# Unit 0's q and k loaded in fp32 by two hardware queues and cast on VectorE, and its first keys copied by themselves

## The chip, the cores and the metric

The kernel runs on one core of one Trainium2 chip. The metric is the time of one execution on the device in microseconds (us). Times are given as the median of several executions; the profile shows one execution.

## What is computed

Two steps follow each other. First attention without a softmax, over 8 batches, 12 heads, 448 positions and 64 numbers a head; then a feed-forward layer over the 3584 rows that come out:

```python
scores = scale * np.matmul(q, k.transpose(0, 1, 3, 2))     # scale = 1/sqrt(64)
attn = np.maximum(scores, 0.0) ** 2 / S                    # S = 448
x = np.matmul(attn, v)                                     # then (B*S, H*D) = (3584, 768)
r = np.maximum(x @ w_in, 0.0)                              # w_in (768, 2048)
out = (r * r) @ w_out                                      # w_out (2048, 768)
```

All inputs and the output are fp32 in HBM. The kernel computes in fp16 with fp32 sums in PSUM.

## The kernel before

**Tiling.** The attention is cut into 24 units, three to a batch; a unit is four heads. Its q, k and v each lie in SBUF as a tile of 128 partitions by 2 by 448 numbers (`heads`, L80): two of the four heads are on the partition axis, the other two (`hh`) beside each other, and each partition holds seven (`J`) positions. A tile of scores is one of the seven groups of keys of a unit, against all 448 queries.

**Loads.** `load16` (L90) loads q and k of a unit on the queue of POOL, which turns fp32 into fp16 on the way; `load_v` (L97) does so for v, `load_w1` and `load_w2` for the weights. POOL's queue holds nearly all loads of the kernel, in program order: first q and k of unit 0 (L153), then the identity matrix that the transposes need (L155, made on POOL too), then units 1 and 2. The queue of SP has the DMA transposes of units 6 and up and the stores of the output; its first instruction comes at 59.8 us.

**The start.** TensorE (PE) runs ten matmuls on zeros (`warm(10)`, L790), then `pe_transpose(0)` (L791): 14 small transposes for q into one PSUM slot, a VectorE (DVE) copy to qT, one more matmul on zeros, the same for k and kT, and one more matmul on zeros. After that the loop of 11 visits (L792) computes the scores of batch 0. `score` (L246) issues the matmuls of a tile, twice each in this stage, and a Relu on ScalarE (ACT, L258) from PSUM to the tile `at`; DVE squares `at` in place (L371), and `av_round` (L262) multiplies it with v.

**PSUM slots.** `slot` (L194) hands out three buffers in turn, every third being `third`; whoever writes a slot waits until the buffer's last user has been read.

**Order.** Nothing reorders the work: the engines run their instructions in the order in which this program issues them. After the first batch a list of steps and events with planned times (L838 and on) fixes that order when the kernel is built. `pe_transpose` is also called for units 1, 2 (two visits of the first loop), 3 (its copies are put off and called as `later`), 4 and 5 (through `mm_tile` buffers).

Of the kernel before, what the change touches and what calls it, by code (L numbers as in the profile page):

```python
# [10 lines left out]
FP16 = mybir.dt.float16  # L11
FP32 = mybir.dt.float32
# [5 lines left out]
def kernel(  # L18
# [9 lines left out]
    nc = tc.nc  # L28

    B, H, S, D = q.shape  # L30
# [11 lines left out]
    P = 128  # L42
    J = 7
# [21 lines left out]
    x_p = ctx.enter_context(tc.tile_pool(name="xp", bufs=3))  # L65
    g_p = ctx.enter_context(tc.tile_pool(name="gp", bufs=1))
    early = ExitStack()
    q16_p = early.enter_context(tc.tile_pool(name="q16p", bufs=3))

    PSUM = bass.MemoryType.PSUM  # L70
# [9 lines left out]
    def heads(t, n):  # L80
        b, u = divmod(n, NU)
        return t[b].rearrange(
            "(hh u hp) (p j) d -> u (hp p) hh (j d)", hh=2, hp=2, j=J)[u]
# [6 lines left out]
    def load16(n):  # L90
        tq = q16_p.tile([P, 2, J * D], FP16, name="q16", tag="q16")
        tk = q16_p.tile([P, 2, J * D], FP16, name="k16", tag="k16")
        nc.gpsimd.dma_start(out=tq, in_=heads(q, n))
        nc.gpsimd.dma_start(out=tk, in_=heads(k, n))
        q16s[n] = (tq, tk)

    def load_v(n):  # L97
        t = v_p.tile([P, 2, J * D], FP16, name="vt", tag="vt")
        nc.gpsimd.dma_start(out=t, in_=heads(v, n))
        vts[n] = t  # L100
# [12 lines left out]
    def new_qkt():  # L113
        return [qkt_p.tile([P, J, P], FP16, name=nm, tag=nm) for nm in ("qT", "kT")]
# [35 lines left out]
        dst, x, y = ((t1, b12, b11), (t3, b22, b12), (t2, b22, t1), (nt4, b21, t2))[op]  # L150
        nc.vector.tensor_sub(dst[:, c], x[:, c], y[:, c])

    load16(0)  # L153
    ident = const_p.tile([P, P], FP16, name="ident", tag="ident")
    make_identity(nc, ident)  # L155
    zeros = const_p.tile([P, S], FP16, name="zeros", tag="zeros")
    nc.vector.memset(zeros, 0.0)
    junk = const_p.tile([P, 1], FP16, name="junk", tag="junk")
    nc.scalar.activation(out=junk, in_=zeros[:, 0:1], func=AF.Relu)
    load16(1)  # L160
    load_v(0)
    load16(2)
# [31 lines left out]
    def slot(dtype):  # L194
        slot_no[0] += 1
        third = not big and slot_no[0] % 3 == 2 and slot_no[0] < 29
        return (third_p if third else s_p).tile(
            [P, 2, 2048 // mybir.dt.size(dtype)], dtype, name="slot", tag="slot")

    def warm(n):  # L200
        ps = slot(FP32)
        for _ in range(n):
            nc.tensor.matmul(ps[:, 0, 0:S], lhsT=zeros[:, 0:P], rhs=zeros,
                             start=True, stop=True)

    def pe_transpose(n):
        srcs = q16s.pop(n)
        ts = new_qkt()
        ps = None if n > 3 else slot(FP16)

        def copy(i, act=False):
            dst, ps = ts[i].rearrange("p j c -> p (j c)"), pss[i][:, i if n < 4 else 0, 0:J * P]
            if act:
                nc.scalar.activation(out=dst, in_=ps, func=AF.Copy)
            else:
                nc.vector.tensor_copy(dst, ps)

        if n > 3:
            pss = [mm_tile(None, FP16).rearrange("p (i c) -> p i c", i=1) for _ in range(2)]
        else:  # L220
            pss = [ps, slot(FP16) if n == 0 else ps]
        for i, src in enumerate(srcs):
            for j in range(J):
                for hh in range(2):
                    nc.tensor.transpose(  # L225
                        pss[i][64 * hh:64 * hh + 64, i if n < 4 else 0, j * P:(j + 1) * P],
                        src[:, hh, j * D:(j + 1) * D], ident)
            if n == 0:
                copy(i)
                warm(1)  # L230
        qkt[n] = ts
        if n == 3:
            return lambda: (copy(0, True), copy(1))
        if n > 0:
            copy(0, n > 3)
            copy(1)


    xts: dict = {}
# [133 lines left out]
    def visit(tiles, turn=None, lag=2, most=3):  # L373
        now[0] += 1
        for t in tiles:
            if t % J == 0 and t >= NPE * J:
                prefetch(t // J + 2)
        if big:
            for t in tiles[:1]:
                score(t)  # L380
            av_unit()
            for t in tiles[1:]:
                score(t)
            at_pe[0] += 0.19 + 0.19 * len(tiles)
            for i, t in enumerate(tiles):
                square(ats[t], 0.6 + 0.85 * i)
            return
        for t in tiles:
            score(t, 2)
        if turn is not None:  # L390
            pe_transpose(turn)
        flush()
        av_some(lag, most)
        for t in tiles:
            square(ats[t])
        flush()
# [5 lines left out]
    def mm_tile(i=None, dtype=FP32):  # L402
        if i is None:
            mm_no[0] += 1
            i = mm_no[0] % len(big)
        return big[i].tile(
            [P, 2048 // mybir.dt.size(dtype)], dtype, name="mm", tag="mm")
# [381 lines left out]
    NB0 = NU * J  # L789
    warm(10)  # L790
    pe_transpose(0)  # L791
    for i in range(11):  # L792
        visit([t for t in (2 * i, 2 * i + 1) if t < NB0], turn={1: 1, 4: 2}.get(i))
# [9 lines left out]
        if i == 5:  # L803
            load16(5)
            load_w1(3)
            load_v(5)
    later = pe_transpose(3)
    load_v(6)
    load_w2(b11, 0, 0)
# [7 lines left out]
        name="mma", bufs=2, space=PSUM, reuse_waits="tile")))  # L817
# [5 lines left out]
    def some(part):  # L823
# [9 lines left out]
        name="mmb", bufs=2, space=PSUM, side="right", reuse_waits="tile")))  # L833
# [36 lines left out]
    for pr in range(1, B // 2):  # L870
# [3 lines left out]
        for i in range(21):  # L874
            ts = [t0 + 2 * i, t0 + 2 * i + 1]
# [86 lines left out]
```

## Time and profile before

| | us |
|---|---|
| median of 3 runs | 373.85 (373.79 to 373.89) |
| the profiled execution | 373.79 |
| its span in the profile | 372.0 |
| PE busy in the span | 361.2 (97%) |
| DVE busy | 278.6 (75%) |
| ACT busy | 247.6 (67%) |
| POOL busy | 107.6 (29%) |

The span runs from the first to the last instruction of the profile; the 1.79 us between it and the execution's time lie around it. PE is busy nearly throughout, but a matmul that waits in the pipeline counts as busy, so the share alone does not say what sets the end. For that there is the chain of waits: it starts at the last instruction and goes back, at each step, to what released it. Lines of the profile give a start, a length and what ran (engine, line of the kernel, operation, tile written <- tiles read, partitions x elements, type, count); the brackets hold the idle time before it and what ended that.

### The profile page before, as it was taken

Reading aid. Unit: us, or ns where it says so; the run is one execution under the profiler, and the core shown is the slowest. Engines: PE = TensorE matmul, PEld = TensorE weight load, DVE = VectorE, ACT = ScalarE, POOL = GpSimd, SP = SyncE. Lnnn points to the kernel's source line nnn. Section 1 sums busy time; section 2 is a strip of 40 time slices with the busy share of each in tenths; the row PEclk is TensorE's granted clock in tenths of the full one; section 3 lists DMA queues with packets and bytes.
Section 4 is the critical chain, followed back from the end, with each engine's and each line's share of the span. In section 5 each row is a group of like instructions: output and inputs, shape, how many; then the busy total and the mean of one; then the engine's idle time right before and its main releaser. Section 6 shows DMA issues by size and latency. Waiting matters only on the chain.

```text
span 372.0 us, 8794 instructions
## 1 busy us (share of the span) xinstructions
PE 361.2 (97%) x3600; PEld 230.4 (62%) x3600; DVE 278.6 (75%) x518; ACT 247.6 (67%) x370; POOL 107.6 (29%) x128
## 2 busy tenths in 40 slices
PE   7999999999999999999999999999999999999994
PEld 3554444445555778875555588786455689975663
DVE  1886677996766787798975668989956688995442
ACT  2997895786676999876556588886665885532220
POOL 8635431955442354432054145140000000000001
PEclk9999999999999999999999999999999999999998
DMA  7999999999999999998798999591233300002333
GB/s 113 203 205 205 205 204 172 134 172 136 171 171 131 174 100 102 115 107 65 137 125 121 186 154 89 82 116 35 55 82 87 86 0 2 2 0 73 95 90 85
DMA packets 121160, 42.65 MB, mean 115 GB/s; under 512 B 100832, under 2 KB 117760, under 8 KB 121120
## 3 DMA queue, kind: packets, MB, share of 16 engines
q0 software_dynamic: 82912, 23.01, 61.7%
q1 hardware_dynamic: 38048, 18.98, 26.8%
q8 instruction: 28, 0.46, 0.5%
q10 hardware_dynamic: 160, 0.10, 0.1%
q14 instruction: 12, 0.10, 0.1%
HBM read 45.61 MB, written 11.01 MB: 152 GB/s over the span
## 4 chain that ended last, share of the span: by engine, by line
PE 84%; DVE 7%; ACT 5%; issue 2%; DMA 1%; POOL 0%; POOLq 0%; DVEq 0%; ACTq 0%
PE mm L739 31%; PE mm L552 25%; PE mm L422 9%; PE slot L254 9%; PE slot L319 7%; ACT at L258 4%; DVE at L371 2%; DMA k<-in_k_dram 1%; DVE s L608 1%; DVE g L500 1%; PE slot L225 1%; DVE g L493 1%; DVE xt L285 1%; DVE osb L646 1%; DVE g L498 1%
## 5 line engine op out<-in xcount | busy, mean ns | idle before, releaser
L258 ACT ACTIVATE at<-slot 128x896 f16<-128x896 f32 x168 | 146.0, 920 | 27.9 <-PE slot L254 27.9
L371 DVE TENSOR_TENSOR at<-at 128x896 f16<-128x896 f16 x168 | 99.0, 617 | 11.2 <-ACT at L258 11.0
L108 POOL DMA_DIRECT2D qs<-in_q_dram x36 | 35.5, 987 | 115.6 <-DMA qT<-qs 107.7
L739 PEld LDWEIGHTS <-s 128*128 128x128 f16 x440 | 41.3, 98 | 34.2 <-DVE s L608 3.8
L254 PE MATMUL slot<-qT,kT 64*64 64x448 f16 x756 | 57.4, 360 | 1.7 <-ACT at L258 0.9
L552 PEld LDWEIGHTS <-w 128*128 128x128 f16 x576 | 54.3, 98 | 5.2 <-issue 4.3
L552 PE MATMUL mm<-xt,w 128*128 128x224 f16 x432 | 49.0, 259 | 0.0
L739 PEld LDWEIGHTS <-g 128*128 128x128 f16 x336 | 31.7, 98 | 24.1 <-issue 4.7
L552 PEld LDWEIGHTS <-ws 128*128 128x128 f16 x432 | 40.3, 98 | 4.7 <-issue 4.7
L739 PE MATMUL mm<-b,g 128*128 128x384 f16 x224 | 40.7, 326 | 0.0
L739 PE MATMUL mm<-b,s 128*128 128x384 f16 x216 | 39.6, 327 | 1.0 <-DVE s L608 0.9
L422 PE MATMUL mm<-xt,w 128*128 128x448 f16 x192 | 39.8, 354 | 0.0
L646 DVE SCALAR_TENSOR_TENSOR osb<-mm,u 128x384 f32<-128x384 f32 (+1 forms) x30 | 16.2, 542 | 31.2 <-ACT u L641 19.3
L739 PE MATMUL mm<-t,s 128*128 128x384 f16 x224 | 39.4, 326 | 0.0
L108 POOL DMA_DIRECT2D ks<-in_k_dram x36 | 35.4, 985 | 9.3 <-DMA b<-in_moe_w_out_dram 5.8
L254 PEld LDWEIGHTS <-kT 64*64 64x64 f16 x756 | 19.6, 104 | 28.9 <-issue 23.6
L575 POOL DMA_DIRECT2D out_dram<-osb x2 | 1.1, 564 | 121.0 <-DVE osb L646 121.0
L641 ACT ACTIVATE u<-mm 128x384 f32<-128x384 f32 x28 | 13.8, 491 | 32.5 <-PE mm L739 31.3
L552 PE MATMUL mm<-x,ws 128*128 128x224 f16 x288 | 34.1, 259 | 0.0
L319 PE MATMUL slot<-at,vt 64*64 64x448 f16 x588 | 31.9, 350 | 0.2 <-DVE at L371 0.2
L500 DVE TENSOR_TENSOR g<-g 128x896 f16<-128x896 f16 x48 | 29.8, 620 | 1.2
L493 DVE TENSOR_TENSOR g<-mm,m 128x448 f16<-128x448 f32 x36 | 22.2, 620 | 10.7 <-PE mm L552 7.4
(69 smaller groups left out, 392.7 us busy)
## 6 DMA issues: line engine op xcount, KB each, us to landing
out_dram<-osb SPq DMA_DIRECT2D x52, 192.0 KB, 3.0
vt<-in_v_dram POOLq DMA_DIRECT2D x24, 224.0 KB, 6.7
qs<-in_q_dram POOLq DMA_DIRECT2D x36, 112.0 KB, 4.3
ks<-in_k_dram POOLq DMA_DIRECT2D x36, 112.0 KB, 5.4
w<-in_moe_w_in_dram POOLq DMA_DIRECT2D x8, 384.0 KB, 11.9
b<-in_moe_w_out_dram POOLq DMA_DIRECT2D x4, 768.0 KB, 17.2
q<-in_q_dram POOLq DMA_DIRECT2D x6, 224.0 KB, 7.1
k<-in_k_dram POOLq DMA_DIRECT2D x6, 224.0 KB, 7.6
```

What stands on the lines that cost most here:

```text
L108: nc.gpsimd.dma_start(out=t[:, :, hh, :], in_=heads(src, n)[:, hh].rearrange("p (j d) -> p j d", d=D))
L254: nc.tensor.matmul(ps[c, hh, 0:S], lhsT=kT[r, j, c], rhs=qT[r, :, c], start=True, stop=True)
L258: nc.scalar.activation(out=at, in_=ps[:, :, 0:S], func=AF.Relu, scale=SK)
L319: nc.tensor.matmul(ps[64 * hh:64 * hh + 64, hp, 0:S], lhsT=vt[r, hh, j * D:(j + 1) * D], rhs=at[r, hh, :], start=(j == 0), stop=(j == J - 1))
L371: lambda: nc.vector.tensor_mul(at, at, at), 0))
L422: nc.tensor.matmul(cell[0][:, 0:S], lhsT=w1[f // 4][:, m, (f % 4) * P:(f % 4 + 1) * P], rhs=xts[b][:, m, :], start=(m == 0), stop=(m == NM ...
L493: nc.vector.tensor_add(gs(s, hi, right), acc(s, y), keep[s, nm])
L500: due_g.append((t, 0.54, lambda: nc.vector.tensor_mul(g, g, g), b))
L552: nc.tensor.matmul(XY[s][y][:, r * Q:(r + 1) * Q], lhsT=left(k, i0 + 2 * s + r, m), rhs=right(k, m), start=(fresh and r == 0 and m == 0), ...
L641: nc.scalar.activation(out=t, in_=X[0][:, 0:HALF], func=AF.Copy, scale=CO)
L646: nc.vector.scalar_tensor_tensor(out=osb[row][:, c], in0=acc[0][:, 0:cc.stop - cc.start], scalar=CO, in1=keep[nm][:, cc], op0=ALU.mult, op ...
L739: nc.tensor.matmul(acc[0][:, 0:HALF], lhsT=left()[:, f], rhs=right[:, f], start=(fresh and f == 0), stop=(f == KH - 1), skip_group_check=n ...
```

## The change

Three things are changed, all ahead of the first score.

1. POOL no longer loads q and k of unit 0. SP loads q and ACT loads k, each as fp32 into a tile of its own (`raw0`, 128 x 896 numbers, a pool of 3.5 KB a tile and partition), and two DVE copies cast them to the fp16 tiles that the transposes read.
2. For unit 0 the keys are transposed in two parts: the first of the seven groups into one slot, the other six into the next slot, with a DVE copy of 128 columns and one of 768 in place of one of 896. One matmul on zeros behind kT's copy is gone; the number of slots taken is the same.
3. `pe_transpose` is written anew around two inner functions, `turn` and `copy`. For the units after 0 it issues the same instructions as before.

```diff
+    raw0_p = early.enter_context(tc.tile_pool(name="raw0p", bufs=1))
     q16_p = early.enter_context(tc.tile_pool(name="q16p", bufs=3))
...
-    load16(0)
+    raw0 = []
+    for src, nm, eng in ((q, "rq", nc.sync), (k, "rk", nc.scalar)):
+        raw0.append(raw0_p.tile([P, 2, J * D], FP32, name=nm, tag=nm))
+        eng.dma_start(out=raw0[-1], in_=heads(src, 0))
     ident = const_p.tile([P, P], FP16, name="ident", tag="ident")
     make_identity(nc, ident)
     zeros = const_p.tile([P, S], FP16, name="zeros", tag="zeros")
     nc.vector.memset(zeros, 0.0)
     junk = const_p.tile([P, 1], FP16, name="junk", tag="junk")
     nc.scalar.activation(out=junk, in_=zeros[:, 0:1], func=AF.Relu)
+    q16s[0] = [q16_p.tile([P, 2, J * D], FP16, name=nm, tag=nm) for nm in ("q16", "k16")]
+    for t, src in zip(q16s[0], raw0):
+        nc.vector.tensor_copy(t, src)
     load16(1)
...
-            if n == 0:
-                copy(i)
-                warm(1)
...
+        if n == 0:
+
+            pq, pk = slot(FP16)[:, 0], slot(FP16)[:, 0]
+            turn(0, pq)
+            copy(0, pq)
+            warm(1)
+            turn(1, pk, slice(0, 1))
+            copy(1, pk, slice(0, 1))
+            pk = slot(FP16)[:, 0]
+            turn(1, pk, slice(1, J))
+            copy(1, pk, slice(1, J))
+            return None
```

`turn(i, ps, js)` issues the two transposes of each group in `js` for q (i = 0) or k (i = 1) into the slot `ps`; `copy(i, ps, js)` copies those columns to qT or kT. Every line of the kernel behind this start moves down by 20 in the profile of the changed kernel (the Relu of the scores is L278 there, the transposes are L230, the copies L225, the casts L167).

## Prediction

> **What bounds the kernel now.** The chain of waits shows two things. First its summary by engine on the page.
>
> ```profile
> PE 84%; DVE 7%; ACT 5%; issue 2%; DMA 1%; POOL 0%; POOLq 0%; DVEq 0%; ACTq 0%
> ```
>
> TensorE carries 84%. DMA has 1%, which is 4.19 us of 372.0, and that is one step, seen in the same chain in order of time for the first 20 us (start, length, what):
>
> ```profile
> 1.28 0.51 POOL q L93
> ...
> 2.12 4.19 DMA k<-in_k_dram
> 6.32 0.04 issue
> 6.36 0.60 PE slot L225 x14
> ...
> 6.99 0.64 DVE kT L216
> ...
> 7.67 0.60 PE slot L254 x8
> ...
> 8.29 6.66 ACT at L258 x8
> ```
>
> So the run begins with load k, transpose k, copy k, first score, first Relu at 8.29; eight Relus then follow without a pause, and later no transfer stands on the chain. The change edits only what lies before 8.29. If the first Relu moves by x, I let the end move by x: behind it the chain goes from ACT to PE and DVE work that the change leaves in the same order, and from 58 us it is matmul after matmul.
>
> Third, the timeline of the start: what the load step is made of.
>
> ```profile
> 0.74 1.28 ACT L159 ACT_TABLE_LOAD   x1 [0.74 <-PEq L946]
> ...
> 1.16 3.86 PE L203 MATMUL slot<-zeros 128*128 128x448 f16 x10 [1.16 <-DVE zeros L157]
> 1.28 0.85 POOL L93 DMA_DIRECT2D q<-in_q_dram  x1 [0.83 <-POOLq L946]
> ...
> 5.27 0.58 PE L225 MATMUL slot<-ident,q 128*64 128x128 f16 x14 [0.25 <-DMA q<-in_q_dram]
> ...
> 5.89 0.62 DVE L216 COPY qT<-slot 128x896 f16<-128x896 f16 x1 [4.79 <-PE slot L225]
> ```
>
> The ten warming matmuls fill PE to 5.02; q has landed by 5.27, k by 6.31. Fourth, the stages in half microseconds (the last two columns are the DMA share and the GB/s written):
>
> ```profile
> 2.50:3.00 0.50, 0.50 (x2) 0.15 (x1) 0.00 (x0) 0.00 (x0) 0.50 (x2) 1.00 0.79 20
> 3.00:3.50 0.50, 0.50 (x3) 0.28 (x2) 0.00 (x0) 0.00 (x0) 0.42 (x3) 1.00 0.26 7
> 3.50:4.00 0.50, 0.50 (x3) 0.18 (x2) 0.00 (x0) 0.00 (x0) 0.50 (x1) 1.00 0.94 147
> 4.00:4.50 0.50, 0.50 (x3) 0.15 (x1) 0.00 (x0) 0.00 (x0) 0.50 (x2) 1.00 1.24 202
> ```
>
> Bytes come from 2.84 on, at a crawl for 0.65 us, then at 200 GB/s of fp16. The queue wrote 23.01 MB where HBM read 45.61, so that is 400 GB/s of fp32 read. Summing the windows, q's 0.229 MB are written by 4.70 and k's by 5.8; each is usable 0.5 to 0.57 us later.
>
> **The change, part by part.** It removes POOL's two loads of unit 0, adds one load each on SP and ACT, adds two DVE casts, splits the copy of kT in two, and drops one of the 12 warming matmuls. In the built order of all five engines nothing else differs; the spread squares that its description names are not in it.
>
> *When q and k land (T).* SP and ACT are free at 0.70 (ACT's table load starts at 0.74). The trace has no load issued there, but a store from SP:
>
> ```profile
> 358.43 9.57 SPq L575 DMA_DIRECT2D out_dram<-osb  x10
> ...
> 359.20:359.45 0.25, 0.25 (x3) 0.17 (x2) 0.24 (x1) 0.00 (x0) 0.00 (x0) 1.00 0.00 0
> 359.45:359.70 0.25, 0.25 (x4) 0.14 (x2) 0.25 (x1) 0.00 (x0) 0.00 (x0) 1.00 0.70 172
> ```
>
> Issue to first bytes is 1.0 to 1.25 us; POOL's load took 1.56 (1.28 to 2.84). I take 1.15. The slow beginning of the reads is bounded by 0 and 0.65; I take 0.65, since it was seen on loads of these very tensors. The data is twice as large on the SBUF side, 2 x 0.459 MB. At the 400 GB/s that the casting loads read it takes 2.3 us; at 250, a good stretch of stores, 3.7. I take 2.3, the row that reads the same rows of HBM. Landing adds 0.55.
>
> Then the neighbour. POOL now makes the identity first (0.60 us in the trace, 2.84 to 3.44), so it issues unit 1's q at about 1.85 instead of 3.40, and this reaches its full rate 2.2 us later, as unit 0's did (1.28 to 3.5), at 4.05. From 2.5 to 4.05 the two new loads have read 0.62 MB; the remaining 0.30 MB share the engines with a third stream: at two thirds of 400 they take 1.1 us instead of 0.75. Bounds: nothing, if the new loads go first; 0.65, if POOL issues at 1.28. I take 0.35.
>
> T = 0.70 + 1.15 + 0.65 + 2.3 + 0.35 + 0.55 = 5.7 for both. In sum k comes 0.6 earlier than now, q 0.45 later.
>
> The Trainium skill (DMA: Bandwidth & Descriptors, Latency and other measured facts) gives about 0.6 us to the first byte for a load issued by SP or ACT, against the 1.15 from the store row. By the page T would be an estimated 5.15 and the sum below a gain of 0.2 us.
>
> *The casts.* No DVE instruction of the trace reads fp32 from SBUF alone. DVE rows with two fp16 inputs give 617 ns for 896 elements and 949 for 1536: 0.519 ns an element and 152 ns fixed. fp32 from PSUM, 448 in 0.62, is 1.04 an element, so 1.09 us for 896 is the upper bound; 0.38, the fp16 tile of L498 from SBUF, is the lower. From PSUM to SBUF the fp16 price per element halves (617 and 383 less 152: 465 to 231). Halving 1.04 gives 0.62 us. I take that.
>
> POOL writes load descriptors all through this time, so I look for a DVE copy from SBUF beside such an issue:
>
> ```profile
> 121.05 2.28 POOL L108 DMA_DIRECT2D ks<-in_k_dram  x2
> ...
> 121.15 0.68 DVE L593 COPY g<-g 128x2048 f16<-128x2048 f16 x1
> ...
> 158.06 0.46 DVE L498 TENSOR_SCALAR g<-g 128x448 f16<-128x448 f16 x1
> ```
>
> L593 kept its 0.68 while POOL's pair took 2.28 where 1.95 is usual; L498 took 0.46 instead of 0.27 beside a load of v. So DVE pays 0 to 0.2 and POOL about 0.3 a copy. POOL's queue runs 1.5 us ahead of before, which covers that; without the cover it would be 0.6 on loads of units 1 and 2 that no one waits for. I take 0.
>
> The Trainium skill (SBUF — State Buffer, Who interferes with whom) speaks against the change: such a copy and POOL's descriptor writing lock each other out for a whole instruction. Were the casts the ones to wait, an estimated 0.7 us each would come on top.
>
> *From T to the first Relu.* Behind the waiting casts are queued on DVE the copies of qT and kT, on PE the transposes and all scores; ACT's first work waits for those. Cast q T+0.05 to T+0.67; cast k, 0.54 later as back-to-back copies start, to T+1.21. PE transposes q from T+0.71; its copy begins 0.62 later (5.27 to 5.89), T+1.34 to T+1.96; the one pair of k and the warming matmul go under it. The other 12 transposes of k need the PSUM buffer that qT's copy frees: from T+2.0, 0.028 us apart, 0.33. The copy of the first keys (128 elements, 0.22) is done meanwhile. Score at T+2.33, Relu 0.62 later (7.67 to 8.29): T+2.95. Before it was k's landing + 1.98 (6.31 to 8.29). So the chain after the landing grows by 0.97 and break-even is T = 5.34. The second copy of kT (0.55) ends at T+3.13, the second score at T+3.79, when the first Relu (0.83) ends at T+3.78: hidden, but with no slack. The dropped warming matmul (0.2 to 0.4) waited beside kT's copy and saves nothing. ACT's issue of about 0.5 delays its table load to 1.25 to 2.5, still 6 us early; SP has no work before 59 us.
>
> Sum: 5.7 + 2.95 - 8.29 = +0.36 us. The profiled run is 373.79 (span 372.0 and 1.79 around it), 0.06 under the median of 373.85: 374.2 us.
>
> **The rivals.**
>
> *Hardware queues win* (0.17): no slow beginning, or q lands first because SP is served before ACT. For it: the store row shows none. T = 0.70 + 1.0 + 2.3 + 0.5 = 4.5 at best: 7.45 against 8.29, -0.84, 373.0; with 0.35 of sharing 373.4. PE's warming to 5.02 then also holds the transposes (T+0.71 = 5.21, just free).
>
> *Data at the stores' rate* (0.15), the main one on the slower side: at 250 GB/s instead of 400 the same 0.92 MB take 3.7, T = 7.1 with sharing, 6.75 without: +1.4 to +1.8, 375.3 to 375.6. It decides from T = 6.1 on, where the loss passes 0.75 us. Against it: stores write HBM, these loads write SBUF.
>
> *Casts at one element a step* (0.10): 1.09 each moves the copy of qT from T+1.34 to T+2.17: +0.83 more, +1.2, 375.05.
>
> *PE cools down* (0.03): silence from 5.02 to T+0.71 = 6.4 is 1.4 us. After the last matmul, at 367.0, the granted clock fell only at 370.05, so it needs T over 7.3; then 375.5 or more.
>
> **How the numbers follow.** The forecast has 0.55, own range 373.5 to 374.6 (sharing and slow beginning at their ends). 0.2%, 0.75 us, is about what a measurement of this kernel can tell from no change. Faster by more needs nearly the whole best case: 0.10 of the first rival's 0.17. Slower by more: 0.15 + 0.10 + 0.03, and 0.04 of the forecast's tail: 0.32. Within: 0.58. The range for 8 in 10 cuts the worst part of the data rival and the tip of the gain: 373.1 to 375.3.
>
> **What would show it.** In the changed profile: DVE's first cast near 5.75 and 0.62 long; the first Relu near 8.65; DMA windows near 400 GB/s by 2.5, shared from 4. Wrong if the cast starts before 5.0 or after 6.1, takes over 0.8, or if the first Relu's shift does not reach the end.

## The result and the profile after

| | before | after |
|---|---|---|
| median, us | 373.82 (373.78 to 373.89, 4 runs) | 375.18 (374.60 to 375.70, 4 runs) |
| ratio | | 1.0036, 95% interval 1.0018 to 1.0053 |
| profiled execution, us (span) | 373.79 (372.0) | 375.41 (373.6) |

The change makes the kernel slower by 1.36 us, and its runs lie 1.1 us apart where those of before lay within 0.11 (in the larger sets taken beside the runs below, those of before lie 0.55 to 0.87 us apart). The chain by engine hardly moves; the loss is all at the start. First that summary, then the chain of the changed kernel in order of time up to 14 us (start, length, what):

```profile
PE 85%; DVE 7%; ACT 4%; issue 2%; DMA 1%; POOL 0%; POOLq 0%; DVEq 0%; ACTq 0%
```

```profile
0.74 4.71 DMA rq<-in_q_dram
...
5.48 0.90 DVE q L167
6.39 0.72 DVE k L167
7.10 0.60 DVE qT L225
...
7.74 0.53 PE slot L230 x12
8.27 3.11 PE slot L274 x32
11.37 1.08 PE slot L230 x28
12.46 0.53 PE slot L274 x8
...
13.01 1.73 ACT at L278 x2
```

q's load is over at 5.46, and k's, which nothing waits for, at 0.75 + 5.0 = 5.75, 0.56 us ahead of k's old landing at 6.31. That sum is from the list of loads (the last number is the time from issue to landing):

```profile
rq<-in_q_dram SPq DMA_DIRECT2D x1, 448.0 KB, 4.7
rk<-in_k_dram ACTq DMA_DIRECT2D x1, 448.0 KB, 5.0
```

But where the kernel before went straight into eight Relus at 8.29, here 32 score matmuls stand on the chain for 3.11 us. Before, 24 of them took 1.33. The timeline of the same stretch:

```profile
0.74 0.45 SPq L158 DMA_DIRECT2D rq<-in_q_dram  x1
0.75 0.48 ACTq L158 DMA_DIRECT2D rk<-in_k_dram  x1
...
5.48 0.90 DVE L167 CAST q<-rq 128x896 f16<-128x896 f32 x1 [4.38 <-DMA rq<-in_q_dram]
...
6.31 0.80 DVE L167 CAST k<-rk 128x896 f16<-128x896 f32 x1
...
6.44 0.58 PE L230 MATMUL slot<-ident,q 128*64 128x128 f16 x14 [1.39 <-DVE q L167]
...
8.20 3.17 PE L274 MATMUL slot<-qT,kT 64*64 64x448 f16 x32
...
9.14 3.35 ACT L278 ACTIVATE at<-slot 128x896 f16<-128x896 f32 x4 [6.38 <-PE slot L274]
```

and its stages (busy time of PE, of PEld, which is TensorE loading weights, of DVE, ACT and POOL, then granted clock, DMA share and GB/s):

```profile
5.00:6.40 1.40, 0.05 (x1) 0.00 (x0) 0.92 (x2) 0.00 (x0) 1.40 (x3) 1.00 1.21 196
6.40:8.30 1.90, 1.61 (x33) 1.12 (x37) 1.42 (x3) 0.00 (x0) 0.97 (x2) 1.00 1.26 201
8.30:11.70 3.40, 3.40 (x40) 1.37 (x41) 1.81 (x3) 2.56 (x4) 2.71 (x4) 0.50 1.27 203
11.70:13.00 1.30, 1.30 (x42) 0.99 (x41) 0.50 (x1) 0.79 (x1) 0.66 (x1) 0.99 1.26 202
```

TensorE is silent from 5.05 to 6.44, and from 8.30 to 11.72 it is granted half its clock. In the kernel before the clock opened at 4.83, that is, went to full, and fell only at 370.05, behind the last matmul.

Put side by side from the two traces, Relu by Relu: the first four are 0.85 us late, the fifth (13.01 for 11.59) 1.42, and from there to the last ACT instruction the shift stays between 1.41 and 1.42, but for one instruction. So the start passes through to the end whole, and nothing later gains or loses. The remaining 0.2 of the 1.6 us between the spans lies behind the issue of the last stores (368.19 for 366.78); no run here says why.

### The profile page after: what moved, and what is told of

Same layout as the page of the kernel before. It is cut to its first block, busy times and chain, and to the rows that moved or that the text cites. A ratio compares the mean times of both kernels' runs of the same rounds, so it can differ in the third digit from the quotient of the medians.

```text
span 373.6 us, 8797 instructions
## 1 busy us (share of the span) xinstructions
PE 362.5 (97%) x3599; PEld 230.4 (62%) x3599; DVE 280.3 (75%) x521; ACT 247.8 (66%) x370; POOL 105.3 (28%) x126
## 4 chain that ended last, share of the span: by engine, by line
PE 85%; DVE 7%; ACT 4%; issue 2%; DMA 1%; POOL 0%; POOLq 0%; DVEq 0%; ACTq 0%
PE mm L759 31%; PE mm L572 25%; PE slot L274 10%; PE mm L442 9%; PE slot L339 7%; ACT at L278 3%; DVE at L391 2%; DMA rq<-in_q_dram 1%; DVE s L628 1%; PE slot L230 1%; DVE g L520 1%; DVE g L513 1%; DVE xt L305 1%; DVE osb L666 1%; DVE g L518 1%
## 5 line engine op out<-in xcount | busy, mean ns | idle before, releaser
L278 ACT ACTIVATE at<-slot 128x896 f16<-128x896 f32 x168 | 146.0, 920 | 28.8 <-PE slot L274 28.7
L274 PE MATMUL slot<-qT,kT 64*64 64x448 f16 x756 | 58.5, 369 | 0.8 <-ACT at L278 0.6
```

The lines of the kernel that those rows point to most:

```text
L274: nc.tensor.matmul(ps[c, hh, 0:S], lhsT=kT[r, j, c], rhs=qT[r, :, c], start=True, stop=True)
L278: nc.scalar.activation(out=at, in_=ps[:, :, 0:S], func=AF.Relu, scale=SK)
```

## The experiments

The question was how the 1.42 us divide: late data, slow casts, the split, or the clock. In every profile the clock's changes lie 3.41 us apart, or multiples of it, but their place against the kernel's start differs from one profile to the next. So each run tells of its own case, and the medians mix them. Ratios are to runs of the kernel before that were taken beside each run; their medians are 373.97 for the runs with 16 warming matmuls, the split alone and the loads alone, 373.78 for the silence by itself and for q on SP with k on POOL, and 373.84 for the others.

**More warming matmuls.**

```diff
-    warm(10)
+    warm(16)
```

> The changed kernel with 16 warming matmuls in place of 10, so that TensorE is busy until about 6.3 us, when q has been cast. Clock theory: TensorE's silence from 5.04 to 6.44 us makes the clock fall to half from 8.30 to 11.72 us, and this costs 0.3 us up to the first Relu and 0.56 us up to the fifth, 0.87 in all. Then the clock stays up, the first Relu comes near 8.8 us, all later Relus are 0.5 to 0.6 us later than in the kernel before, the time is 374.3 to 374.5 us and the runs agree within 0.2 us. Rival, late data and slow casts alone: the time stays at 375.2 us, with the first Relu at 9.1.

Measured: 374.70 us (374.54 to 375.36), ratio 1.0021 (1.0012 to 1.0031). The median falls by about 0.5 us, though not to 374.4, and the intervals of the two ratios overlap, so the medians alone do not show a gain. In its profile the clock never falls again (all Relus are 0.89 to 0.91 us late, with no jump at the fifth), but it opened only at 6.28:

```profile
1.16 5.71 PE L211 MATMUL slot<-zeros 128*128 128x448 f16 x16 [1.16 <-DVE zeros L162]
...
6.80 0.58 PE L230 MATMUL slot<-ident,q 128*64 128x128 f16 x14
```

With the changed kernel's opening at 4.89 about ten of the sixteen would run slow; here all but the last few did, so the warming itself held q's transposes back from 6.44 to 6.80. A fixed number of matmuls overshoots when the clock opens late.

That filling the silence keeps the clock up is seen in every run's mean granted clock. The two profiles with a fall at the start, the changed kernel's and one below, have 0.995; the kernel before has 0.996 or more in all its runs. Two of the changed kernel's four runs have that value, and none of the 20 runs with 16 warming matmuls here and in the next experiment (0.996 to 1.000).

**The same, with POOL's loads held back.** A write of one column of the fp32 k tile, which must wait for k's cast, stands in POOL's queue behind three loads:

```diff
-    for t, src in zip(q16s[0], raw0):
-        nc.vector.tensor_copy(t, src)
     load16(1)
     load_v(0)
+    for t, src in zip(q16s[0], raw0):
+        nc.vector.tensor_copy(t, src)
+    nc.gpsimd.memset(raw0[1][:, 0, 0:1], 0.0)
     load16(2)
```

> As the run with 16 warming matmuls, and besides POOL holds its loads behind the first three (q, k of unit 1, v of unit 0) until both casts are done, by a write of one column of the fp32 k tile. Lock theory: the casts take 0.62 us each when POOL writes no load descriptors, q's transposes start 0.28 us earlier, the first Relu comes near 8.5 us and the time is 374.1 us. Rival, the cast itself costs 0.8 to 0.9 us: no change against the run with 16 warming matmuls, 374.4 us.

Measured: 374.30 us (374.10 to 375.16), ratio 1.0013 (1.0004 to 1.0022); the profiled run is 374.13. Seven of its eleven runs took 374.10 to 374.33, the other four 374.96 to 375.16; what these four lost is open, since none of them was profiled. Its timeline:

```profile
1.16 5.01 PE L212 MATMUL slot<-zeros 128*128 128x448 f16 x16 [1.16 <-DVE zeros L162]
...
5.49 0.63 DVE L169 CAST q<-rq 128x896 f16<-128x896 f32 x1 [4.38 <-DMA rq<-in_q_dram]
...
6.03 0.62 DVE L169 CAST k<-rk 128x896 f16<-128x896 f32 x1
...
8.55 1.73 ACT L279 ACTIVATE at<-slot 128x896 f16<-128x896 f32 x2 [5.78 <-PE slot L275]
```

The lock theory holds for these casts: with no descriptors being written they take 0.63 and 0.62 us; beside them 0.90 and 0.80. This clock opened at 4.87, in the changed kernel's profile at 4.89, so these two can be laid on each other: same landing, first Relu 0.59 us earlier. q's cast explains 0.28; the rest is the first score, 0.62 us to its Relu here, 0.94 there, where the clock fell under it. From the fifth Relu on the difference is 1.16.

**The casts alone.** As the run above, with the 10 warming matmuls left as they were:

```diff
-    warm(16)
+    warm(10)
```

> The changed kernel with POOL's later loads held until both casts are done, and the 10 warming matmuls as they were. Lock theory: casts of 0.62 us, first Relu 0.3 us or more ahead of 9.14 us; TensorE's silence is shorter by 0.28 us only, so some runs still lose clock: 374.3 to 374.9 us, the runs spread over 0.5 us or more. Rival, the casts cost nothing because late data decides: 375.2 us.

Measured: 375.06 us, ratio 1.0028 (1.0020 to 1.0037), above what was expected. Two of its eleven runs took 374.12 and 374.16, the other nine 374.97 to 375.28: two groups 0.8 to 1.2 us apart. Four of the nine, the profiled run among them, have the mean clock of a fall, 0.995. The other five, 375.15 to 375.28, have 0.997 to 0.999, so no fall is recorded in them; a clock that opened late, as in the next experiment, would not show in this number, and their cause is open. The profiled run's casts took 0.63 and 0.62, and yet its first Relu came at 9.31 instead of 0.3 us ahead of 9.14:

```profile
4.60:6.20 1.60, 0.01 (x1) 0.00 (x0) 0.67 (x2) 0.00 (x0) 0.00 (x0) 1.00 1.16 240
6.20:7.40 1.20, 1.05 (x17) 0.65 (x18) 1.06 (x3) 0.00 (x0) 0.64 (x2) 1.00 1.26 200
7.40:10.80 3.40, 3.28 (x40) 1.80 (x43) 1.29 (x4) 1.49 (x2) 3.40 (x6) 0.50 1.17 172
```

The clock opened early, at 4.00, so the warming ended early, the silence grew to 1.6 us and the clock fell at 7.41. The run before differs in the warming alone, and there the clock stayed up. Mending the casts without the silence is worth little in most runs.

**Silence by itself.** The kernel before, with no new load, cast or split:

```diff
-    warm(10)
+    warm(6)
```

> The kernel before with 6 warming matmuls in place of 10: loads, landings and copies stay as they are, TensorE is silent from 3.5 us to q's landing at 5.27, 1.8 us. Clock theory: with so little work in a stretch of 3.41 us the clock opens later or falls again while the first scores run; 374.3 to 375 us, and the runs spread over 0.5 us or more. Rival, a silence of under 3 us does nothing, since only a long one lowers the clock: 373.85 us with runs as close together as before.

Measured: 375.08 us (374.83 to 376.32), ratio 1.0041 (1.0028 to 1.0053). The clock theory holds and its rival falls: the landings are those of before (q's transposes start at 5.32, for 5.27), and four warming matmuls fewer, with a silence of 1.73 us, cost as much as the whole change.

```profile
1.16 2.42 PE L203 MATMUL slot<-zeros 128*128 128x448 f16 x6 [1.16 <-DVE zeros L157]
...
5.32 0.96 PE L225 MATMUL slot<-ident,q 128*64 128x128 f16 x14 [1.73 <-DMA q<-in_q_dram]
...
8.38 2.45 PE L254 MATMUL slot<-qT,kT 64*64 64x448 f16 x24 [0.24 <-DVE kT L216]
...
9.39 1.73 ACT L258 ACTIVATE at<-slot 128x896 f16<-128x896 f32 x2 [7.14 <-PE slot L254]
```

The way is another one, though: here the clock did not fall, it first opened at 11.00. 24 score matmuls took 2.45 us instead of 1.33.

How busy TensorE was in the 3.41 us that ended where the clock might have fallen or did (stages of the profiles):

| run | stretch, us | PE busy, us | what followed |
|---|---|---|---|
| POOL held, 10 warming | 4.00 to 7.41 | 1.66 | clock fell |
| changed kernel | 4.89 to 8.30 | 1.77 | clock fell |
| loads only (below) | 5.69 to 9.10 | 2.24 | stayed |
| both loads on SP (below) | 3.92 to 7.33 | 2.46 | stayed |
| before | 4.83 to 8.24 | 2.52 | stayed |
| POOL held, 16 warming | 4.87 to 8.28 | 3.16 | stayed |

The other four profiles whose clock opened by 6.28 had 2.54 to 3.01 us, and it stayed. So in these runs what keeps the clock up lies between 52% (1.77) and 66% (2.24) of one such stretch, busy as the profile counts it, transposes included. The length of the silence does not decide: the run with the loads alone was silent for 1.36 us, nearly as long as the changed kernel, but only 0.75 us of that fell into its stretch:

```profile
6.44 0.58 PE L233 MATMUL slot<-ident,q 128*64 128x128 f16 x14 [1.36 <-DVE q L167]
```

Opening took more than staying open. With 6 warming matmuls two stretches with 2.42 us (71%) and 2.27 us (67%) busy passed before the clock opened; with both loads on SP, 2.76 us (81%), from 0.51 to 3.92, opened it.

The Trainium skill (TensorE: Matmul & The Clock Gate, Part 1: The HAM clock gate) says that activity is judged over free-running windows of about 3.4 us; the 3.41 us here agree, and so does the scatter of where they begin. Its rule for authors (the same page, Why this matters for your kernels) is to leave no gap above about 3 us; here 1.4 was enough, and the measurement decides.

**The split alone, and the loads alone.** First the kernel before with the new `pe_transpose`:

```diff
-            if n == 0:
-                copy(i)
-                warm(1)
...
+            turn(1, pk, slice(0, 1))
+            copy(1, pk, slice(0, 1))
+            pk = slot(FP16)[:, 0]
+            turn(1, pk, slice(1, J))
+            copy(1, pk, slice(1, J))
```

> The kernel before with the new pe_transpose alone: POOL loads q and k as before, the first keys are copied by themselves and the last warming matmul is gone. If the split is worth what the chain says, the score starts near 6.95 us (k landed at 6.31, first pair and its copy of 0.22 us, the other 12 transposes behind qT's copy), the first Relu at 7.6 us instead of 8.29, and the time is 373.1 to 373.2 us. Rival: the second copy of kT makes the second Relu late by as much as the first is early, and the time stays at 373.8 us.

Measured: 373.46 us (373.09 to 373.90), ratio 0.9987 (0.9979 to 0.9996). The split is a gain, of 0.5 us instead of 0.7. Its profiled run has the clock opening at 6.13, and then the warming is what the start waits for, with the first Relu at 7.87:

```profile
1.16 3.91 PE slot L203 x10
...
5.11 0.98 PE slot L222 x14
...
6.12 0.64 DVE qT L217
...
6.79 0.53 PE slot L222 x12
7.32 0.53 PE slot L266 x8
...
7.87 1.73 ACT at L270 x2
```

Then the changed kernel with the old `pe_transpose` (the diff above, reversed):

> The changed kernel with the old pe_transpose: fp32 loads and casts, but kT copied in one piece and with the last warming matmul. Theory that the loads and casts are the loss and the split a gain: the first Relu comes near 9.5 us, 0.3 to 0.4 us later than in the changed kernel, and the time is 375.5 to 376 us, with the clock falling as in the changed kernel. Rival, the split is the loss: the time goes back towards 373.8 to 374.3 us.

Measured: 374.97 us (374.56 to 376.69, seven runs), ratio 1.0038 (1.0022 to 1.0054). The loss comes with the loads and casts. That it is no larger than the whole change was not expected; the profiled run kept its clock (2.24 us busy in the table), and with the kT copy in one piece its first Relu was at 9.17. How much the missing split costs here can't be read from runs spread over 2 us.

**Both fp32 loads on one queue.**

```diff
-    for src, nm, eng in ((q, "rq", nc.sync), (k, "rk", nc.scalar)):
+    for src, nm, eng in ((q, "rq", nc.sync), (k, "rk", nc.sync)):
```

> The changed kernel with both fp32 loads on SP's queue, q first, k behind it. In the changed kernel SP's first bytes came 1.0 us after its issue, ACT's 2.0 us after, then both shared the engines and both had landed only at 5.4 us. Theory that the sharing costs: q alone reads its 0.46 MB by 3.6 us and lands near 4.2, k near 5.4; q's cast and transposes then lie under k's load, TensorE's silence behind the warming nearly goes, the clock stays up, the first Relu comes near 7.9 us and the time is 373.4 to 373.6 us. Rival, the order within the transfers does not matter because the last landing decides: 374.6 to 375.2 us as for the changed kernel.

Measured: 373.80 us (373.47 to 373.95), ratio 0.9995 (0.9986 to 1.0003): all that the change lost comes back. In the changed kernel, q alone moves first, on SP's queue (q1), and then shares the engines with ACT's (q10) for two microseconds; the lines of its queues (packets, MB, share) from 1.5 to 2.7 us, then from 2.7 to 4.7:

```profile
q1 hardware_dynamic: 42, 0.08, 55.5%
...
q1 hardware_dynamic: 217, 0.37, 51.2%
q10 hardware_dynamic: 197, 0.35, 47.1%
```

On one queue q no longer shares:

```profile
4.21 0.75 DVE L167 CAST q<-rq 128x896 f16<-128x896 f32 x1 [3.10 <-DMA rq<-in_q_dram]
...
5.01 0.42 PEld L230 LDWEIGHTS <-q 128*64 128x64 f16 x14 [0.88 <-DVE q L167]
...
5.42 0.63 DVE L167 CAST k<-rk 128x896 f16<-128x896 f32 x1 [0.47 <-DMA rk<-in_k_dram]
...
7.72 0.92 ACT L278 ACTIVATE at<-slot 128x896 f16<-128x896 f32 x1 [5.48 <-PE slot L274]
```

q lands at 4.2 instead of 5.46, and k at 5.4 instead of 5.75; q's cast goes under the warming, and TensorE, whose warming ended at 4.57 in this run, takes up q at 5.01. The expected median (373.4 to 373.6) was missed; the profiled run, at 373.53, had the earliest clock of all.

**One load by SP, one by POOL.** First k by SP, transposed first and copied by ACT, with q on POOL:

```diff
+    rk = raw0_p.tile([P, 2, J * D], FP32, name="rk", tag="rk")
+    nc.sync.dma_start(out=rk, in_=heads(k, 0))
+    nc.gpsimd.dma_start(out=q16s[0][0], in_=heads(q, 0))
...
+            turn(1, pk)
+            copy(1, pk, act=True)
+            warm(1)
+            turn(0, pq)
+            copy(0, pq)
```

> Only k is loaded in fp32, by SP, and cast on VectorE; q is loaded and cast by POOL's queue as in the kernel before. k is transposed first and copied in one piece by ACT, then q, copied by VectorE. Theory: k lands near 4.1 us, q at 5.3 to 5.6 us, a single landing decides and it is q's, one microsecond ahead of k's old one; first Relu near 7.5 us, time 373.0 to 373.2 us. Rival, the two queues push each other back as in the changed kernel: q lands at 6 us, first Relu at 8.2, time 373.7 to 373.9 us.

Measured: 374.00 us (373.46 to 375.30), ratio 1.0003 (0.9993 to 1.0012): no gain. The rival was right about the transfer: POOL's q came at 6.04, 0.8 us later than in the kernel before. Its first bytes came at 3.64 instead of 2.84, though POOL issued it at 1.27 as before (1.28); what is new until then is SP's fp32 load.

```profile
6.04 0.58 PE L228 MATMUL slot<-ident,q 128*64 128x128 f16 x14 [0.15 <-DMA q<-in_q_dram]
...
7.96 1.73 ACT L274 ACTIVATE at<-slot 128x896 f16<-128x896 f32 x2 [1.41 <-PE slot L270]
```

Then the reverse, q by SP and k on POOL, with the keys split as in the change:

```diff
+    rq = raw0_p.tile([P, 2, J * D], FP32, name="rq", tag="rq")
+    nc.sync.dma_start(out=rq, in_=heads(q, 0))
+    nc.gpsimd.dma_start(out=q16s[0][1], in_=heads(k, 0))
...
+    nc.vector.tensor_copy(q16s[0][0], rq)
```

> Only q is loaded in fp32, by SP, and cast on VectorE; k is POOL's first load, cast on the way; keys split as in the change. From the runs so far: q alone on SP is cast by 5.0 us, POOL's load beside one fp32 load landed near 6.0 us. Theory that each part is worth what its own chain says: q's transposes at 5.0 and its copy by 6.2 lie under k's load, k's first pair starts at 6.05, the score at 6.65, the first Relu at 7.3 us, and the time is 372.9 to 373.2 us. Rival, the start is at its floor with the split alone: 373.4 to 373.5 us.

Measured: 373.25 us (372.75 to 373.66), ratio 0.9984 (0.9975 to 0.9993): the fastest median, ahead of both kernels. But the gain over the kernel before, 0.53 us, is that of the split alone, 0.51, so the rival, a start that is at its floor with the split, is not refuted. q was out of the way by 6.4; but POOL's k came at 6.66 in the profiled run, later than the 6.05 expected, and the first Relu at 7.90:

```profile
1.27 5.39 DMA k<-in_k_dram
...
6.70 0.58 PE slot L228 x14
7.28 0.59 PE slot L272 x8
...
7.90 1.73 ACT at L276 x2
```

Its timeline also limits the lock theory:

```profile
4.10 0.89 POOL L100 DMA_DIRECT2D vt<-in_v_dram  x1
4.21 0.63 DVE L165 CAST q<-rq 128x896 f16<-128x896 f32 x1 [3.11 <-DMA rq<-in_q_dram]
```

Here the cast kept its 0.63 us beside an issue of POOL, and it was the issue that grew, from 0.71 to 0.74 us (this load's time in the kernel before) to 0.89; with k on SP the same happened (cast 0.63, issue 0.93). Which of the two pays differs from case to case, and no run shows what decides it.

## Why the prediction was right, and where it was wrong

The direction of the likeliest sum was right, and 375.18 lies just inside the range of 373.1 to 375.3. That it does is luck: it lies outside the forecast's own range of 373.5 to 374.6, the upper end was put there for the data rival, which did not happen, and the mechanism that made most of the loss was the rival that I had given 0.03. The sum in its own terms, for the profiled run:

| term | predicted | measured | difference to the sum, us |
|---|---|---|---|
| landing, T (q's; k landed at 5.75, off the path) | 5.7 | 5.46 | -0.24 |
| q's cast | 0.62 | 0.90 | +0.28 |
| 12 transposes of k, to the first score | 0.33 | 0.46 | +0.13 |
| first score to first Relu | 0.62 | 0.94 | +0.32 |
| later, to the fifth Relu | 0 | 0.56 | +0.56 |

They sum to +1.05 (rounding aside), and the predicted +0.36 becomes 1.42, the shift seen. The 12 transposes were mis-sized: they took 0.46 in the runs with 16 warming matmuls too, where the clock stayed up.

**The clock: wrong, and most of it.** "PE cools down" was there with the right place (behind the warming) and the right silence (1.4 us), and was put away because after the last matmul the clock fell only 3 us later. That row is one stop, at the end of a stretch; it does not show how short a silence can be enough. 0.32 + 0.56 = 0.88 us of the 1.42 are the clock's: the run with POOL held and 16 warming matmuls, whose clock opened at the same time, did without them. With 10 warming matmuls, the four POOL-held runs that have a fall on record took 0.8 to 0.9 us more than its two fastest.

**The casts: price right, cover wrong.** 0.62 us alone, as the halved row gave. "DVE pays 0 to 0.2 ... I take 0" was the failed step: DVE paid 0.28 and 0.18 beside POOL's descriptor writing, and the 0.90 is over the 0.8 that the prediction had named as a sign of being wrong. The Trainium skill (SBUF — State Buffer, Who interferes with whom), which spoke against the change, was right in kind; the casts were lengthened by 0.28 and 0.18 and did not wait for a whole 0.71 us instruction, and with one load by SP they paid nothing. Only q's added to the path. The chain names k's cast too, but that ended (7.10) at the moment when qT's copy could start anyway, 0.62 us behind q's transposes (6.44), as in the kernel before (5.27 to 5.89).

**The landing: nearly right by errors that cancel.** SP's first bytes came at 1.86, 1.1 us after the issue, close to the 1.15 taken, and the slow beginning came too (0.08 MB until 2.7), but ACT's came at 2.83, 2.1 after a simultaneous issue. Against that, the sharing with POOL's load, put at 0.35, hardly happened: POOL issued it at 1.47, earlier than the 1.85 assumed, but its bytes began only at 4.85, 3.4 us later. The data rival is refuted (364 GB/s from 2.7 to 4.7 us, not 250), and so is "hardware queues win" in this form: 5.46 and not 4.5. For a load from SP the Trainium skill (DMA: Bandwidth & Descriptors, Latency and other measured facts) has about 0.6 us to the first byte; both queues here were slower.

**The split and the pass-through.** The split, which the prediction did not price by itself, is worth 0.5 us, and, as assumed, a shift at the first Relu reaches the end unchanged: 1.42 at the fifth, 1.41 at the last.

## What to carry to other kernels

A step that waits for data at the start of a kernel has a second price: if TensorE falls silent behind its warming, the clock can drop and the next microseconds run at half speed, so check that the warming reaches the first real work in every phase of the clock, not in one profile. Two transfers that are both needed should follow each other on a queue when work on the first can start alone; side by side the first landed 1.2 us later here and the second no earlier (5.46 for 4.2, 5.75 for 5.4). A cast moved from a DMA queue to VectorE is priced beside whatever POOL writes at that moment, and the first piece of an operand that is copied by itself can be worth more than a faster load.

## What the runs showed of the hardware

- The clock is judged in stretches of 3.41 us that do not begin with the kernel: in ten of the eleven profiles it first opened at 3.92 to 6.28 us, and at 11.00 in the one with 6 warming matmuls. The granted clock is shown as 1.00 until the first change is recorded, also while matmuls on zeros still come 0.373 us apart.
- A DVE cast of 128 x 896 from fp32 in SBUF takes 0.62 us. Beside POOL's issuing of loads it took 0.90 in the changed kernel, and 0.63 in two other runs, where POOL's issue grew from 0.71 to 0.74 us to 0.89 and 0.93 instead.
- Of two loads issued together by SP and ACT, ACT's began 1.0 us after SP's. Why, and why POOL's load beside them began 3.4 us after its issue instead of 1.56, was not tried.
